# Attention and gated feed-forward in one kernel: two projection units placed ahead of the last token block's first one, and seven early scores instead of three

## The chip, the cores and the metric

The kernel runs on one core of one Trainium2 chip. The metric is device time in microseconds (us) of the whole program: 1323.13 us before the change, the median of three runs (1322.75 to 1323.53).

## The reference

The inputs are x (2048 tokens of 448 numbers), the attention weights wqkv (448 x 1344) and wo (448 x 448), the feed-forward weights W_gate and W_up (448 x 1792) and W_down (1792 x 448), and a gate vector gate_w, all float32. Cut to what matters:

```python
q, k, v = split(x @ wqkv)                      # 16 heads of 28
p = softmax(q @ k.T * 28 ** -0.5)
a = (p @ v) @ wo
b = ((relu(x @ W_gate)) * (x @ W_up)) @ W_down
g = sigmoid((x * gate_w).sum(-1))
out = g * a + (1 - g) * b
```

## The kernel before

Products that need float32 accuracy are made of float32r parts. A weight or activation is split into a high part (a ScalarE copy, `act_high`, L81) and a low part (the rest, a VectorE subtraction, `low`, L87), and each product is eleven matmuls (`TERMS`) that add high and low parts of the four slices of the 448 rows. The order on every engine is written out by hand: the instructions run on each engine in the order in which the code issues them.

**The projection stage** works in units. `qk(tb, c)` (L239) makes 128 columns (chunk c of 7) of q and k for a block tb of 512 tokens (4 blocks): eleven matmuls of 512 columns into a PSUM bank, a high copy on ScalarE and a low part on VectorE into the SBUF tile `st` (3 buffers), and one DMA on POOL's queue that writes both to `qk_d` in DRAM (512 KB). `vproj(tb, t)` (L248) makes v for 128 tokens, eleven matmuls of 450 columns, and ScalarE copies the result and the gate's sum (`zt`) out of PSUM. The bank of a unit comes from `ps_any`, which turns through four: the two banks of the tag `s`, then one of `x` and one of `po`. The weights come in chunks (`load_w` on SP's queue, two buffers; `split_w` on ScalarE and VectorE), the tokens' x in blocks (`load_x`, `split_x`: X0 to X3).

**The code around the change** first issues the units (0,0), (0,1), (1,0), (1,1), (0,2), (2,0) and (3,0) one by one, between the loads and splits. (3,0) is the first that reads X3. Then come the split of the fourth weight chunk, the load of the last one to come (`load_w(3)`), and `load_k(0)` and `load_q(0)`, the eight DMAs on SP's queue that bring head 0's K and Q back from `qk_d`, each copied to four groups of partitions; they need chunk 0 of all four blocks. The rest stands in a list, `mixed`: first (2,1), (1,2) and (3,1), then qk units and vproj units in turn, and it ends with (3,6), v(0,2), (2,6), v(0,3), (1,6), (0,6). Before given places of the list stand two weight splits, the loads of head 1's K and Q, and the spills of x to DRAM (`spill_x`).

From a given unit on, `smax` steps follow the units. `smax(k)` (L130) multiplies 128 queries by 1024 keys in two matmuls into one of two double banks, and VectorE takes the maxima, which the exponentials need. 48 of a total of 512 such steps run in this stage.

**Scores.** `scores(i, j)` (L159) is one matmul of 128 keys (tile i: head i // 16, key tile i % 16) by 512 queries (block j) into one of the two banks of the tag `s`, and the exponential on ScalarE into `PT[i]`, one of five buffers in SBUF, which hold X1, X2 and half of X3 until those have been read for the last time. After each of the last three units one score, s(0,0) to s(0,2), is issued ahead of the `smax` steps. s(0,3) follows behind the list.

**The rounds.** 64 rounds follow, each of which issues 16 scores, `smax` steps (8 in most rounds) and some feed-forward matmuls (`gu_mm`) by a string (`ROUND`: s, m and x), and then `pv` for four key tiles: 4 x 4 narrow matmuls that multiply the exponentials by v. Round 0 has no feed-forward matmuls; its scores are those of the tiles 1 to 4. After the rounds come the rest of the feed-forward part, the output projection and the down projection.

The list as it is built before:

```python
        units = [(qk, 2, 1), (qk, 1, 2), (qk, 3, 1), (qk, 2, 2), (qk, 3, 2)]
        units += [(qk, tb, c) for c in range(3, NQ) for tb in range(NB - 1, -1, -1)]
        vs = [(vproj, tb, t) for tb in range(NB - 1, -1, -1) for t in range(4)]
        mixed = units[:3]
```

Of the kernel before, what the change touches and what calls it, by code (L numbers as in the profile page):

```python
# [27 lines left out]
NB = 4  # L28
# [3 lines left out]
VC = D + 2  # L32
NQ = 2 * D // P
WARM = 13


LEAD = 24
# [18 lines left out]
def gated_mix_kernel(ctx, tc, x, wq, wo, wgu, wd, out):  # L56
# [8 lines left out]
    def f32(ap):  # L65
        return ap.bitcast(F32)

    def ps_s(name):
        return psum.tile([P, TB], F32, tag="s", bufs=2, name=name)
# [4 lines left out]
    def ps_o(name):  # L74
        return psum.tile([P, TB], F32, tag="po", bufs=1, name=name)

    def ps_x(name):
        return psum.tile([P, TB], F32, tag="x", bufs=1, name=name)

    def act_high(dst, src):  # L80
        nc.scalar.activation(dst, src, AF.Copy)  # L81
# [4 lines left out]
    def low(dst, src, high):  # L86
        nc.vector.tensor_tensor(dst, src, f32(high), op=OP.subtract)  # L87
# [19 lines left out]
    def p_slot(name, dt=F32):  # L107
        return vp.tile([P, 4, TB], dt, name=name, tag="P", bufs=PB + 1)
# [9 lines left out]
    def load_k(h):  # L118
        for r in range(4):
            nc.sync.dma_start(f32(K[h % 3])[DH * r:DH * (r + 1)], qk_d[r % 2, 2 * DH * h:2 * DH * h + DH, :])  # L120

    def load_q(h):
        Q[h] = q_slot(f"Q_{h}").rearrange("p j t -> p (j t)")
        for r in range(4):
            nc.sync.dma_start(f32(Q[h])[DH * r:DH * (r + 1)], qk_d[r // 2, 2 * DH * h + DH:2 * DH * (h + 1), :])
# [4 lines left out]
    def smax(k):  # L130

        h, u, half = maxima[k]
        if u == 0 and half == 0:
            MX[h] = keep.tile([P, 32], F32, name=f"mx_{h}", tag="mx", bufs=2)
        ps = ps_w(f"sm_{k}")
        for c in range(2):
            k0 = (half * 2 + c) * TB
            nc.tensor.matmul(ps[:, c, :], Q[h][:GD, u * P:(u + 1) * P], K[h % 3][:GD, k0:k0 + TB],  # L138
                             start=True, stop=True)
        nc.vector.tensor_reduce(MX[h][:, 2 * u + half:2 * u + half + 1], ps, axis=AX.XY, op=OP.max)  # L140
        if u == NK - 1 and half == 1:
            M[h] = keep.tile([P, 16], F32, name=f"m_{h}", tag="m", bufs=2)
            nc.vector.tensor_reduce(M[h], MX.pop(h).rearrange("p (a b) -> p a b", b=2), axis=AX.X, op=OP.max)
# [15 lines left out]
    def scores(i, j):  # L159
        h, kt = divmod(i, NK)  # L160
        if j == 0:
            PT[i] = p_slot(f"P_{i}")
        ps = ps_s(f"s_{i}_{j}")
        nc.tensor.matmul(ps, K[h % 3][:GD + 2, kt * P:(kt + 1) * P], Q[h][:GD + 2, j * TB:(j + 1) * TB],  # L164
                         start=True, stop=True)
        nc.scalar.activation(PT[i][:, j], ps, AF.Exp, scale=SCALE)  # L166
# [3 lines left out]
    def xf(tb, b):  # L170
        return X[tb][b // 4][:, b % 4]


    with tc.tile_pool(name="qkv", bufs=1) as pa:
        W = pa.tile([P, 7, 2 * D + VC], F32R, name="W")

        def load_w(c):
            c0, c1 = c * 2 * GD, (c + 1) * 2 * GD if c < G + 1 else 2 * D + VC
            wr = pa.tile([P, 4, 2 * GD + 2], F32, name=f"wr_{c0}", tag="wr", bufs=2)[:, :, :c1 - c0]
            nc.sync.dma_start(wr, wq[:, :, c0:c1])  # L180
            return wr, c0, c1

        def split_w(wr, c0, c1):

            ways = [(W[:, :, c0:c1], wr)]
            if c0 < 2 * D:
                w, r = (ap.rearrange(f"p c {n} -> p c a j d", a=2, j=4)
                        for ap, n in ((W[:, :, c0:c1], "(j a d)"), (wr, "(a j d)")))
                ways = [(w[:, :, a], r[:, :, a]) for a in range(2)]
            for w, r in ways:  # L190
                act_high(w[:, 0:3], r[:, 0:3])
                low(w[:, 3:6], r[:, 0:3], w[:, 0:3])
            for w, r in ways:
                act_high(w[:, 6], r[:, 3])
                low(w[64:, 6], r[64:, 3], w[64:, 6])
# [34 lines left out]
        def spill_x(tb, r):  # L230
            nc.gpsimd.dma_start(x_d[tb, r], f32(X[tb][r]))
# [3 lines left out]
        def ps_any(name):  # L235
            turn[0] += 1
            return (ps_s, ps_s, ps_x, ps_o)[turn[0] % 4](name)

        def qk(tb, c, terms=TERMS):  # L239
            ps = ps_any(f"qk_{tb}_{c}")  # L240
            for n, (a, b) in enumerate(terms):
                nc.tensor.matmul(ps, W[:, a, c * P:(c + 1) * P], xf(tb, b), start=(n == 0), stop=(n == NT - 1))  # L242
            st = pa.tile([P, 2, TB], F32R, name=f"st_{tb}_{c}", tag="st", bufs=3)
            act_high(st[:, 0], ps)
            low(st[:, 1], ps, st[:, 0])
            nc.gpsimd.dma_start(qk_d[:, c * P:(c + 1) * P, tb * TB:(tb + 1) * TB].rearrange("r d t -> d r t"), f32(st))
# [20 lines left out]
        ps = ps_o("warm_ps")  # L267
        for n in range(WARM):
            nc.tensor.matmul(ps, warm[:, :P], warm, start=True, stop=True)
# [26 lines left out]
        w4 = load_w(4)  # L296
        qk(2, 0)
        w5 = load_w(5)
        qk(3, 0)
        split_w(*w4)  # L300
        w3 = load_w(3)
        load_k(0)
        load_q(0)

        units = [(qk, 2, 1), (qk, 1, 2), (qk, 3, 1), (qk, 2, 2), (qk, 3, 2)]
        units += [(qk, tb, c) for c in range(3, NQ) for tb in range(NB - 1, -1, -1)]
        vs = [(vproj, tb, t) for tb in range(NB - 1, -1, -1) for t in range(4)]
        mixed = units[:3]
        units = units[3:]
        while units or vs:  # L310
            mixed += units[:1] + vs[:1]
            units, vs = units[1:], vs[1:]
        m, first = 0, 8
        spills = {16 + 3 * k: (NB - 1 - k // 2, k % 2) for k in range(6)}
        for n, (f, *a) in enumerate(mixed):
            if n == 1:
                split_w(*w5)
            if n == 3:
                split_w(*w3)
            if n == 6:  # L320
                load_k(1)
                load_q(1)
            if n in spills:
                spill_x(*spills[n])
            f(*a)
            if n >= len(mixed) - 3:
                scores(0, n + 3 - len(mixed))
            while m < 2 * LEAD and n >= first and m < (n + 1 - first) * 2 * LEAD / (len(mixed) - first):
                smax(m)
                m += 1  # L330
                if m == 2 * NK + 3:
                    smax_end(0)
# [59 lines left out]
    NI = H * NK  # L392
# [61 lines left out]
    fetch_f(1)  # L454
    load_k(2)
    load_q(2)
    scores(0, NB - 1)
    for r in range(NR):
        h, q = divmod(r, NK // PB)
        order = ROUND if r < LAST_M else LATE  # L460
        todo = list(range(nxt, min(nxt + (0 if r == 0 else 1 if r < LAST_M else 2), 2 * done)))
        nxt += len(todo)
        if r in X_ROUNDS:
            load_x_split(*X_ROUNDS[r])

        if q == 0 and h and h + 2 < H:
            load_k(h + 2)
            load_q(h + 2)
        if r == 1:
            gates()  # L470
        if r == 2:
            pack_wo()
        if r < LAST_M and m in range(2 * NK, len(maxima), 2 * NK):
            smax_end(m // (2 * NK) - 1)
        if r == LAST_M:
            smax_end(H - 1)
        if h and q == 1:
            row_sums(h - 1)
            spread(h - 1)
        if h and q == 2:  # L480
            normalise(h - 1)
        ns = nx = 0
        for o in order:
            if o == "s":
                i, j = PB * r + 1 + ns // NB, ns % NB
                if i < NI:
                    scores(i, j)
                ns += 1
            elif o == "m":
                smax(m)  # L490
                m += 1
            elif nx < NT * len(todo):
                i, half = divmod(todo[nx // NT], 2)
                if nx % NT == 0:
                    ps = ps_x(f"gu_{i}_{half}") if r < LAST_M else ps_w(f"gu_{i}_{half}")[:, 0]
                gu_mm(ps, i, half, nx % NT)
                nx += 1
                if nx % NT == 0:
                    (spill_h if half else relu)(i, ps)

        ready = min(nxt + (2 if r + 1 < LAST_M else 3), 2 * done + 2)
        while parts < ready:
            split_f(parts // 2, pool_low, (parts % 2,))
            parts += 1
            if parts % 2 == 0:
                fetch_f(parts // 2 + 1)
        if r == LAST_M:
            wor = load_wo()
        for i in range(PB * r, PB * (r + 1)):
            pv(i)  # L510
            if i == NI - NK // 2:
                split_wo(wor)
# [105 lines left out]
    n = todo.index((gate_up, (NB - 1) * NF))  # L618
# [50 lines left out]
```

## Time and profile before

| What | Value |
|---|---|
| Median of three runs | 1323.13 us |
| The profiled execution's own time | 1323.03 us |
| Its span, first to last instruction | 1321.3 us |
| TensorE busy (PE) | 1313.3 us, 99% |
| VectorE (DVE), ScalarE (ACT) | 815.3 us (62%), 772.6 us (58%) |
| GpSimd (POOL) | 307.0 us, 23% |
| Granted TensorE clock | 1.00 |
| The projection stage | up to about 142 us |
| Round 0 | about 142 to 156 us |

One execution was recorded. PE is the matmuls, PEld the weight loads beside them, SPq and POOLq the issuing of DMAs on the queues of SP and POOL. A row of the timeline gives the start and the length of a run of equal instructions in us, the engine, the line, the tiles written and read, how many there are, and in brackets how long the engine was idle before it and what ended that. Ends of matmuls are modelled, and one row may overlap the next. A row of the windows gives the busy time of each engine in that stretch with its instructions in brackets, then the granted clock, the share of the DMA engines that was busy, and GB/s. A row of the waits gives who waited for whom, the time in total, how often, and the longest.

### The profile page before, as it was taken

What the parts mean: (1) busy time and instruction counts of PE and PEld (TensorE: products, weight loads), DVE (VectorE), ACT (ScalarE), POOL (GpSimd) and SP (SyncE); (2) the same over time, 40 slices, a digit from 0 to 9 for tenths busy, and PEclk for the clock granted to TensorE, in tenths of its full rate; (3) what the DMA queues carried; (4) which work ended last, traced back from release to release, by engine and by line L of the source; (5) the groups of instructions that cost most, each with busy time, mean ns of one, the idle gap of its engine ahead of it and who ended that gap; (6) DMA issues with size and microseconds to landing.
All of it is one profiled execution on the core that took longest, in us unless ns stands there. A gap on an engine that the chain in (4) does not pass through costs nothing.

```text
span 1321.3 us, 17544 instructions
## 1 busy us (share of the span) xinstructions
PE 1313.3 (99%) x6689; PEld 894.3 (68%) x6689; DVE 815.3 (62%) x859; ACT 772.6 (58%) x1454; POOL 307.0 (23%) x434
## 2 busy tenths in 40 slices
PE   9999999999999999999999999999999999999998
PEld 5888656656656566566566566565655788888997
DVE  6567867767767767677677677677600456633342
ACT  5212667767767777777677677677788332322121
POOL 3111112131121212222221221312325332301120
PEclk9999999999999999999999999999999999999999
DMA  8744622313223151331324313231122674433432
GB/s 298 263 171 180 175 62 61 81 48 99 56 71 88 40 152 57 89 88 40 88 86 123 77 51 81 61 92 32 50 91 79 209 265 149 163 121 120 133 113 78
DMA packets 50013, 144.67 MB, mean 109 GB/s; under 512 B 9544, under 2 KB 16648, under 8 KB 44808
## 3 DMA queue, kind: packets, MB, share of 16 engines
q1 hardware_dynamic: 33640, 96.70, 25.5%
q0 software_dynamic: 16288, 46.84, 10.2%
q8 instruction: 53, 0.87, 0.3%
q14 instruction: 32, 0.26, 0.1%
HBM read 99.96 MB, written 43.93 MB: 109 GB/s over the span
## 4 chain that ended last, share of the span: by engine, by line
PE 98%; DMA 1%; ACT 0%; DVE 0%; issue 0%; SPq 0%; ACTq 0%
PE gu L374 22%; PE s L164 20%; PE sm L138 19%; PE po L400 17%; PE acc L586 10%; PE qk L242 4%; PE v L251 3%; PE wo L538 3%; DMA xr<-x 1%; DMA qk_d<-st 1%; PE mt L148 0%; ACT X L81 0%; DVE X L87 0%; ACT st L81 0%; ACT P L166 0%
## 5 line engine op out<-in xcount | busy, mean ns | idle before, releaser
L140 DVE TENSOR_REDUCE mx<-sm 128x1 f32<-128x1024 f32 x512 | 606.5, 1219 | 174.9 <-PE sm L138 171.9
L166 ACT ACTIVATE P<-s 128x512 f32<-128x512 f32 x1024 | 583.1, 596 | 168.6 <-PE s L164 109.3
L164 PE MATMUL s<-Q,K 114*128 114x512 f32 x1024 | 419.5, 410 | 0.5 <-ACT P L166 0.5
L138 PE MATMUL sm<-K,Q 112*128 112x512 f32 x1024 | 323.4, 399 | 0.2
L164 PEld LDWEIGHTS s<-Q,K 114*128 114x128 f32 x1024 | 192.1, 188 | 146.8 <-ACT P L166 83.1
L374 PE MATMUL gu<-XF,wg 128*128 128x512 f32 x924 | 270.8, 395 | 0.0
L400 PE MATMUL po<-P,V 128*32 128x512 f32 x2048 | 233.0, 595 | 0.0
L138 PEld LDWEIGHTS sm<-K,Q 112*128 112x128 f32 x1024 | 189.6, 189 | 45.6 <-DVE mx L140 9.9
L374 PEld LDWEIGHTS gu<-XF,wg 128*128 128x128 f32 x924 | 174.6, 189 | 34.1 <-issue 0.8
L90 POOL TENSOR_TENSOR wg<-wgr,wg 128x384 fp32r<-128x384 f32 (+1 forms) x105 | 95.8, 914 | 283.3 <-ACT wg L81 187.5
L400 PEld LDWEIGHTS po<-P,V 128*32 128x32 f32 x2048 | 60.0, 109 | 131.0 <-issue 130.7
L586 PE MATMUL acc<-WD,hh 128*128 128x448 f32 x672 | 141.7, 367 | 0.0
L586 PEld LDWEIGHTS acc<-WD,hh 128*128 128x128 f32 x672 | 126.2, 188 | 12.8
L389 POOL DMA_DIRECT2D h_d<-h x56 | 31.4, 562 | 394.6 <-DVE h L383 188.4
L383 DVE TENSOR_TENSOR h<-gu,rl 128x512 f32<-128x512 f32 x56 | 38.4, 686 | 132.1 <-ACT rl L380 71.1
L380 ACT ACTIVATE rl<-gu 128x512 f32<-128x512 f32 x56 | 33.3, 594 | 128.0 <-PE gu L374 128.0
L374 PE MATMUL gu<-X,wg 128*128 128x512 f32 x308 | 108.0, 395 | 0.0
L87 DVE TENSOR_TENSOR hh<-hr,hh 128x512 fp32r<-128x512 f32 x56 | 55.3, 988 | 51.8 <-ACT hh L81 51.8
L81 ACT ACTIVATE hh<-hr 128x512 fp32r<-128x512 f32 x56 | 35.1, 628 | 74.3 <-PE acc L586 72.4
L242 PE MATMUL qk<-X,W 128*128 128x512 f32 x308 | 76.5, 398 | 1.9 <-ACT X L81 1.6
L81 ACT ACTIVATE wg<-wgr 128x384 fp32r<-128x384 f32 x168 | 72.6, 484 | 0.0
L242 PEld LDWEIGHTS qk<-X,W 128*128 128x128 f32 x308 | 57.4, 189 | 18.0 <-ACT X L81 2.6
(56 smaller groups left out, 596.6 us busy)
## 6 DMA issues: line engine op xcount, KB each, us to landing
wgr<-wgu SPq DMA_DIRECT2D x56, 512.0 KB
qk_d<-st POOLq DMA_DIRECT2D x28, 512.0 KB, 3.7
K<-qk_d SPq DMA_DIRECT2D x64, 224.0 KB
Q<-qk_d SPq DMA_DIRECT2D x64, 224.0 KB
h_d<-h POOLq DMA_DIRECT2D x56, 256.0 KB, 2.3
hr<-h_d SPq DMA_DIRECT2D x56, 256.0 KB
x_d<-X POOLq DMA_DIRECT2D x6, 1024.0 KB, 5.1
XF<-x_d SPq DMA_DIRECT2D x6, 1024.0 KB
```

Of the source, the lines that this page charges most:

```text
L81: nc.scalar.activation(dst, src, AF.Copy)
L87: nc.vector.tensor_tensor(dst, src, f32(high), op=OP.subtract)
L90: nc.gpsimd.tensor_tensor(dst, src, f32(high), op=OP.subtract)
L138: nc.tensor.matmul(ps[:, c, :], Q[h][:GD, u * P:(u + 1) * P], K[h % 3][:GD, k0:k0 + TB], start=True, stop=True)
L140: nc.vector.tensor_reduce(MX[h][:, 2 * u + half:2 * u + half + 1], ps, axis=AX.XY, op=OP.max)
L164: nc.tensor.matmul(ps, K[h % 3][:GD + 2, kt * P:(kt + 1) * P], Q[h][:GD + 2, j * TB:(j + 1) * TB], start=True, stop=True)
L166: nc.scalar.activation(PT[i][:, j], ps, AF.Exp, scale=SCALE)
L242: nc.tensor.matmul(ps, W[:, a, c * P:(c + 1) * P], xf(tb, b), start=(n == 0), stop=(n == NT - 1))
L251: nc.tensor.matmul(ps[:, :VC], xf(tb, b)[:, t * P:(t + 1) * P], W[:, a, 2 * D:], start=(n == 0), stop=(n == NT - 1))
L374: nc.tensor.matmul(ps, WS[i][:, s, a], xf(i // NF, b), start=(n == 0), stop=(n == NT - 1))
L400: nc.tensor.matmul(PO[h][32 * j:32 * j + 32], V[:, kt, h], PT[i][:, j], start=(kt == 0), stop=(kt == NK - 1))
L586: nc.tensor.matmul(ACC[tb][t][:, :D], hh[:, a, t * P:(t + 1) * P], WD[:, f, b], start=(f == 0 and n == 0), stop=(f == NF - 1 and n == 2))
```

## The change

(2,1) and (1,2) are taken from the head of the list and issued ahead of (3,0). The list is two shorter, and the places in it that are given by number (the first `smax`, the spills, the loads of head 1) are two lower, so they stay at the same units. The two weight splits keep their numbers in the list, 1 and 3, and so stand two units later. The early scores are given by a tuple, `EARLY`: entry k is the distance from the end of the list behind whose unit score k is issued. Behind (2,6) stands s(0,0); behind v(0,3) s(0,1) and s(0,2); behind (1,6) s(0,3) and s(1,0); behind (0,6) s(1,1) and s(1,2). Round 0 leaves out the scores that are there already, the first three of its string, and s(0,3) behind the list goes. The number of all instructions is the same.

```diff
+EARLY = (4, 3, 3, 2, 2, 1, 1)
...
         qk(2, 0)
         w5 = load_w(5)
+        qk(2, 1)
+        qk(1, 2)
         qk(3, 0)
         split_w(*w4)
         w3 = load_w(3)
         load_k(0)
         load_q(0)
 
-        units = [(qk, 2, 1), (qk, 1, 2), (qk, 3, 1), (qk, 2, 2), (qk, 3, 2)]
+        units = [(qk, 3, 1), (qk, 2, 2), (qk, 3, 2)]
...
-        mixed = units[:3]
-        units = units[3:]
+        mixed = units[:1]
+        units = units[1:]
...
-        m, first = 0, 8
-        spills = {16 + 3 * k: (NB - 1 - k // 2, k % 2) for k in range(6)}
+        m, first = 0, 6
+        spills = {14 + 3 * k: (NB - 1 - k // 2, k % 2) for k in range(6)}
...
-            if n == 6:
+            if n == 4:
                 load_k(1)
                 load_q(1)
...
-            if n >= len(mixed) - 3:
-                scores(0, n + 3 - len(mixed))
+            for k in range(len(EARLY)):
+                if EARLY[k] == len(mixed) - n:
+                    scores(*divmod(k, NB))
...
-    scores(0, NB - 1)
     for r in range(NR):
...
-                if i < NI:
+                if len(EARLY) <= i * NB + j < NI * NB:
                     scores(i, j)
```

## The prediction

> **What bounds the kernel now.** A unit (tb, c) is `qk` of token block tb and column chunk c, v(tb, t) a `vproj`, s(i, j) a score, m a `smax` (two matmuls and one VectorE maximum). The page comes first:
>
> ```profile
> PE 1313.3 (99%) x6689; PEld 894.3 (68%) x6689; DVE 815.3 (62%) x859; ACT 772.6 (58%) x1454; POOL 307.0 (23%) x434
> ```
>
> TensorE is busy 99% of the span. Every edit here moves work and removes none, so only TensorE's waiting can change. The table of 10 us windows shows where it waits: a full window holds 46 to 48 matmuls, two in the changed stage hold 36.
>
> ```profile
> 20.00:30.00 10.00, 8.42 (x36) 6.13 (x35) 7.29 (x11) 5.37 (x11) 2.90 (x4) 1.00 1.04 395
> ...
> 50.00:60.00 10.00, 10.00 (x47) 8.41 (x46) 6.53 (x6) 1.81 (x5) 1.30 (x2) 1.00 0.77 279
> ...
> 140.00:150.00 10.00, 9.72 (x36) 5.89 (x35) 9.24 (x10) 7.30 (x14) 1.04 (x2) 1.00 0.47 164
> ```
>
> The first is the wait for the last tokens' x, the second is round 0. The granted clock (1.00) is full in all three. Then the timeline by engine, first the early stretch (start, length, instructions, [idle before <- releaser]):
>
> ```profile
> 10.15 13.63 PE L242 MATMUL qk<-X,W 128*128 128x512 f32 x56 [0.16 <-DVE X L87]
> 25.34 13.30 PE L242 MATMUL qk<-X,W 128*128 128x512 f32 x55 [1.55 <-ACT X L81]
> 38.47 2.42 PE L251 MATMUL v<-W,X 128*128 128x450 f32 x11
> ...
> 50.29 1.10 PE L138 MATMUL sm<-K,Q 112*128 112x512 f32 x4
> 27.73 10.47 PEld L242 LDWEIGHTS qk<-X,W 128*128 128x128 f32 x46 [0.46 <-DVE X L87]
> 24.24 2.00 ACT L81 ACTIVATE X<-xr 128x1024 fp32r<-128x1024 f32 x2
> 25.32 2.36 DVE L87 TENSOR_TENSOR X<-xr,X 128x1024 fp32r<-128x1024 f32 x2 [0.25 <-ACT X L81]
> ```
>
> The 55 matmuls from 25.34 are (3,0), (2,1), (1,2), (3,1) and (2,2). (3,0) waits 1.55 us for the high part of X3 and again, at 27.73, for its low part, done at 27.68.
>
> **The change, part one: two units in front of (3,0).** Matmuls start 0.233 us apart ((38.47 - 27.73)/46), a unit takes 2.56 us. Without waiting, a unit could start at 23.62 (the row's end 23.78, less the 0.16 by which ends trail the next start: 38.64 against 38.47). (2,1) and (1,2) need X2 and X1, long there, and fill the time to 28.74, when X3 has been ready for a microsecond. Five units then end at 36.4 instead of 38.47: **2.1 us gained at this place**, and the first m, 50.29 before, could start at 48.2.
>
> What that triggers: (3,0), the last unit that heads 0 and 1 need, now runs from 28.74 to 31.3 and is copied later still, and everything queued behind it moves.
>
> ```profile
> 29.63 0.60 ACT L81 ACTIVATE st<-qk 128x512 fp32r<-128x512 f32 x1 [1.92 <-DMA qk_d<-st]
> 28.72 0.72 POOL L246 DMA_DIRECT2D qk_d<-st  x1 [2.64 <-DVE st L87]
> DMA to landing us min/median/max: 4.1/4.1/4.1
> 31.25 0.72 POOL L246 DMA_DIRECT2D qk_d<-st  x1 [1.80 <-DVE st L87]
> 30.91 1.28 DVE L87 TENSOR_TENSOR W<-wr,W 128x672 fp32r<-128x672 f32 x2
> 17.36 15.40 SPq L180 DMA_DIRECT2D wr<-wq  x3
> 34.89 1.75 SPq L120 DMA_DIRECT2D K<-qk_d  x4
> ...
> 44.86 3.86 SPq L125 DMA_DIRECT2D Q<-qk_d  x4
> SPq L125 <- DMA Q<-qk_d: 3.4, 4, 1.0
> ```
>
> `st` has three buffers, so a unit's copy waits for the write of the unit three before it. (3,0) is now ninth; its copy waits for the sixth unit's write, issued at 28.72 as before and landed 4.1 us later (the row below it), at 32.8. A copy at 32.9 means a write issued 1.62 us later (29.63 to 31.25), at 34.5, landed in 3.6 more (31.25 to K's issue at 34.89, which waited for it), at 38.1. The K and Q loads of head 0, behind it on SP, issue at **38.1 instead of 34.89**. The third weight load moves too: it follows the split of the fourth, whose low part ends at 32.19 now and near 35.4 after, so it stays 2.7 us ahead of K on SP's queue.
>
> When do K and Q land? Head 1's eight loads each wait for the landing of the one eight earlier (the last row), so the last issue, at 48.4 (44.86 + 3.86 - 0.3), is head 0's last landing: 13.5 us after the first issue, and 1.9 us before the first m. From the other side, a later head's loads with nothing beside them:
>
> ```profile
> 247.84 1.62 SPq L120 DMA_DIRECT2D K<-qk_d  x4
> 249.00:250.00 1.00, 1.00 (x6) 0.68 (x5) 0.84 (x2) 0.81 (x3) 0.00 (x0) 1.00 0.68 229
> ...
> 257.00:258.00 1.00, 1.00 (x5) 0.69 (x5) 1.00 (x2) 0.90 (x3) 0.00 (x0) 1.00 0.66 148
> ```
>
> They move bytes until 258: 10.3 us. After the change the load lands between 48.5 and 51.6. I take 12.4 us, nearer the contended row (the same weight load is ahead, and units still write every 5 us, but the backlog of writes is smaller): 50.5. **So the first m starts at 50.5, not 48.2, and the gain is gone: +0.2 us**, bounds -1.7 to +1.3. Behind that waiting m stand all later units on TensorE; ScalarE's copies and VectorE's maxima follow them, so nothing overtakes it.
>
> The lower bound is not -2.1 because v(3,0) has its own wait: the fifth weight split now follows the copy of (3,1), held to 34.9 by the write issued at 31.25. Two copies and the low part (0.6 + 0.7 + 0.86, half a microsecond overlapped) end near 37.0, and the second matmul of v(3,0) wants it at 36.6: 0.4 us, hidden while the K/Q wait is longer. The third weight split, now behind v(3,0), may cost as much again; hidden likewise.
>
> A rule of the Trainium skill speaks against this number (DMA: Bandwidth & Descriptors, Anatomy of one DMA): about 2.0 us fixed plus bytes at 436 GB/s. As an estimate from that page, the eight loads of 224 KB would land 6.2 us after issue, at 44.3, and the gain would stay. The quiet rows (148 to 229 GB/s) do not agree. The same page of the Trainium skill (Queues, rings and completion order) has one ring per engine for SP's queue, consumed in order, and round robin against other queues; by it the weight load in front and the writes beside delay K, as the 13.5 us against 10.3 suggest.
>
> **Part two: seven scores between the last units.**
>
> ```profile
> 128.78 2.72 PE L242 MATMUL qk<-X,W 128*128 128x512 f32 x11
> 131.54 0.60 ACT L81 ACTIVATE st<-qk 128x512 fp32r<-128x512 f32 x1 [2.89 <-PE qk L242]
> 134.54 0.39 PE L164 MATMUL s<-Q,K 114*128 114x512 f32 x1
> 135.18 0.17 ACT L255 ACTIVATE zt<-v 128x1 f32<-128x1 f32 x1
> 141.47 0.40 PE L164 MATMUL s<-Q,K 114*128 114x512 f32 x1
> 142.17 4.87 ACT L166 ACTIVATE P<-s 128x512 f32<-128x512 f32 x8
> 142.81 0.50 PE L164 MATMUL s<-Q,K 114*128 114x512 f32 x1 [0.25 <-ACT P L166]
> 142.91 10.29 DVE L140 TENSOR_REDUCE mx<-sm 128x1 f32<-128x1024 f32 x9
> 151.30 0.63 PE L138 MATMUL sm<-K,Q 112*128 112x512 f32 x2
> 152.59 3.64 PE L400 MATMUL po<-P,V 128*32 128x512 f32 x32
> ```
>
> Round 0 before: the last unit's matmuls end their turn at 141.47, the first `pv` starts at 152.59, 11.1 us for 36 matmuls that need 8.4. Two loops hold it: ScalarE's exponentials, one per 0.6 us through two score banks, and VectorE's nine maxima back to back (1.13 us apart), the first after the last unit's low half. The ninth m needs the bank of the seventh maximum, done at 142.91 + 6 x 1.134 + 1.22 = 150.9; it starts at 151.30. **At most 0.4 us can come out of round 0 by taking scores away.** And that little is used up: with three scores fewer, the first three m stand together, the third waits for the first maximum (144.1) and ends its turn at 144.8; the 13 scores left take 13 x 0.6 = 7.8 us and end at 152.6, as before. After the last unit: 0, bounds -0.4 and +0.1.
>
> Ahead of it the scores cost. The `s` tag has two banks, shared by units and scores; in the program as built s(0,0) takes the one that v(0,3) gets next, and s(0,2) follows v(0,3) in it.
> - Three more scores stand ahead of the end of (0,6): 3 x 0.233 = 0.70.
> - v(0,3) waits for the exponential of s(0,0). That follows the copy of (2,6) on ScalarE (131.54), so it starts near 132.03 and ends at 132.63; the matmuls before v(0,3) (one score, two m, from 131.34) are through at 132.50. 0.2, and 0.1 for restarting (142.81: 0.50 instead of 0.39): 0.3.
> - s(0,2) waits for the copies out of v(0,3), which end 0.81 after TensorE has left it (135.35 against 134.54); it wants to start 0.23 after. 0.6, and 0.1 for restarting: 0.7. The m behind it and the unit (1,6) wait with it.
>
> Sum **+1.7 us**, bounds +1.3 (round 0's 0.4) and +2.0. The copies of (1,6) and (0,6), the writes and the first weight split of the feed-forward part move with the units and wait for nothing new.
>
> **Sum.** The profiled execution took 1323.03 us (span 1321.3), 0.1 below the median of three. 0.2 + 1.7 = 1.9: **1324.9 us**. A later round has 43 matmuls (10.0 us) and its `pv` against eight maxima (9.1), so TensorE sets its length and the shift stays to the end.
>
> **Rivals.**
> 1. The front's gain survives: K and Q land by 48.6 (under 10.5 us; the quiet rows' 10.3 speaks for it, the 13.5 against). -1.7 + 1.7: 1323.0. The Trainium skill's 6.2 us would give this. 13%.
> 2. Clearly slower: the K/Q load is what the new order makes last. If it takes 13.5 us again the first m starts at 51.6, +1.3; with a tail of +2.0, 1326.3. It decides from 13.2 us on (+1.0 with the forecast tail). For it: the weight load stands as far in front as before. Against: fewer writes in flight. 23%.
> 3. Round 0 is ScalarE's after all: three exponentials less (1.8) outweigh three scores (0.7), the new bank waits vanish, and the front keeps 1.7: 1323.03 - 1.1 - 1.7 = 1320.2. The nine maxima without a gap speak against it. 4%.
>
> **How the numbers follow.** Forecast 60%. About 0.2% (2.6 us) is what a measurement of this kernel can tell from no change; the forecast and rival 1 lie within it: same 73%, slower 23%, faster 4%. The range adds the bounds: -1.7 + 1.3 = -0.4, 1322.6; +1.3 + 2.0 = +3.3, 1326.3.
>
> **What would show it.** (a) No wait of TensorE for ACT X or DVE X near 25 us, v(3,0) near 36.5. (b) K's issue on SP near 38 and a wait of 1 to 2 us before the first m, ended by the loads, at 50.5; a start at 48 to 49 refutes step one. (c) Two short waits around v(0,3), the nine maxima again without gap, and 11 us from the last unit to the first `pv`; under 10.5 us refutes step two.

## The result

The changed kernel takes 1329.93 us (median of five runs, 1329.85 to 1330.97) against 1323.25 us (five runs of the kernel before beside them, 1322.75 to 1323.74): ratio 1.0052, 95% interval 1.0038 to 1.0066. It is **6.7 us slower**; the forecast was +1.9 (1324.9 us), the range ended at 1326.3. The profiled execution took 1330.16 us (span 1328.4), 7.1 more than the profiled one of before. Line numbers of the changed kernel are 2 to 5 higher.

The page first: TensorE is busy 99% as before, with the same number of instructions.

```profile
PE 1315.6 (99%) x6689; PEld 895.6 (67%) x6689; DVE 816.1 (61%) x859; ACT 772.9 (58%) x1454; POOL 307.8 (23%) x434
```

The table of 10 us windows shows where that changed. The last three columns are granted clock, DMA share and GB/s.

```profile
20.00:30.00 10.00, 10.00 (x45) 8.14 (x44) 7.56 (x11) 5.30 (x11) 2.71 (x4) 1.00 1.03 387
...
50.00:60.00 10.00, 6.29 (x21) 4.76 (x20) 2.36 (x2) 1.21 (x3) 0.49 (x1) 0.83 0.92 281
...
150.00:160.00 10.00, 8.74 (x32) 4.68 (x35) 10.00 (x10) 7.06 (x14) 0.73 (x1) 1.00 0.65 197
```

The wait for x near 25 us is gone: 45 matmuls instead of 36 in the first window. The second held 47 and now holds 21, and its clock is no longer 1.00. The timeline of TensorE says which instructions:

```profile
9.98 26.36 PE L244 MATMUL qk<-X,W 128*128 128x512 f32 x111 [0.16 <-DVE X L89]
36.66 0.47 PE L253 MATMUL v<-W,X 128*128 128x450 f32 x1 [0.32 <-ACT W L83]
37.56 2.30 PE L253 MATMUL v<-W,X 128*128 128x450 f32 x10 [0.43 <-DVE W L89]
...
47.94 2.42 PE L253 MATMUL v<-W,X 128*128 128x450 f32 x11
54.07 1.55 PE L140 MATMUL sm<-K,Q 112*128 112x512 f32 x4 [3.71 <-DMA K<-qk_d]
55.42 3.92 PE L244 MATMUL qk<-X,W 128*128 128x512 f32 x11
```

Ten units now run in one row without a gap, and v(3,0) starts at 36.66 instead of 38.47. Then the first m stands 3.71 us before its loads and starts at 54.07 instead of 50.29. The unit behind it takes 3.92 us where one took 2.72, and the m itself 1.55 where it took 1.10: together 1.65 us more, and the rows name no engine as the cause. The windows of half a microsecond show it:

```profile
54.00:54.50 0.50, 0.43 (x2) 0.42 (x3) 0.00 (x0) 0.00 (x0) 0.00 (x0) 1.00 1.11 336
54.50:55.00 0.50, 0.50 (x4) 0.36 (x3) 0.19 (x1) 0.00 (x0) 0.00 (x0) 0.63 0.79 246
55.00:55.50 0.50, 0.50 (x3) 0.41 (x2) 0.50 (x1) 0.00 (x0) 0.00 (x0) 0.50 0.94 328
...
57.50:58.00 0.50, 0.50 (x3) 0.35 (x2) 0.00 (x0) 0.00 (x0) 0.00 (x0) 0.50 0.84 336
58.00:58.50 0.50, 0.50 (x4) 0.41 (x3) 0.00 (x0) 0.00 (x0) 0.00 (x0) 0.96 0.94 369
```

**The granted clock falls to half** at 54.63 (0.63 of the half microsecond from 54.5) and is full again at 58.04: 3.4 us. The loads in the timeline, first on SP's queue, then on POOL the writes of four units, from the sixth to the ninth, which is (3,0), then the third weights' split on ScalarE:

```profile
17.04 19.02 SPq L182 DMA_DIRECT2D wr<-wq  x3
39.33 2.25 SPq L122 DMA_DIRECT2D K<-qk_d  x4
...
50.09 4.17 SPq L127 DMA_DIRECT2D Q<-qk_d  x4
```

```profile
29.47 0.73 POOL L248 DMA_DIRECT2D qk_d<-st  x1 [3.60 <-DVE st L89]
32.06 0.73 POOL L248 DMA_DIRECT2D qk_d<-st  x1 [1.86 <-DVE st L89]
33.31 0.73 POOL L248 DMA_DIRECT2D qk_d<-st  x1 [0.53 <-DVE st L89]
34.55 0.73 POOL L248 DMA_DIRECT2D qk_d<-st  x1 [0.51 <-DVE st L89]
```

```profile
41.77 0.48 ACT L83 ACTIVATE W<-wr 128x336 fp32r<-128x336 f32 x1 [1.27 <-DMA wr<-wq]
```

The third weight load, last of the first row, has been issued at 36.06 (17.04 + 19.02) instead of 32.76 and is waited for until 41.77. (3,0)'s write is issued at 34.55 and landed at 39.33, when K may go: 4.8 us, 3.6 before. The weight load has moved with that write: it is through 1.51 us behind the write's start, as before (31.25 to 32.76). New are the two writes 1.24 and 2.49 us ahead of (3,0)'s; before, the nearest stood 2.53 us ahead (28.72). K and Q take 14.7 us from there to the first m; the last issue of head 1's, at 53.96 (50.09 + 4.17 - 0.3), which follows head 0's last landing, says the same.

Last the end of the projection stage, TensorE and then VectorE:

```profile
134.19 2.72 PE L244 MATMUL qk<-X,W 128*128 128x512 f32 x11
...
138.09 2.53 PE L253 MATMUL v<-W,X 128*128 128x450 f32 x11
140.46 0.39 PE L166 MATMUL s<-Q,K 114*128 114x512 f32 x1
141.31 0.50 PE L166 MATMUL s<-Q,K 114*128 114x512 f32 x1 [0.47 <-ACT zt L257]
...
148.60 0.64 PE L166 MATMUL s<-Q,K 114*128 114x512 f32 x2
...
159.73 3.64 PE L405 MATMUL po<-P,V 128*32 128x512 f32 x32
```

```profile
150.03 10.30 DVE L142 TENSOR_REDUCE mx<-sm 128x1 f32<-128x1024 f32 x9
```

The first row is (2,6), 5.41 later than before (128.78). The first `pv`, at 159.73, is 7.14 later (152.59): the tail cost 1.73. From the last unit's turn (148.60) to it are 11.13 us, 11.12 before, with the nine maxima again back to back.

**The account**, against the same points of before: v(3,0) is 1.8 us earlier; the first m is 3.8 later, so that gain is gone; the clock adds 1.65, which makes 5.4 at (2,6); the tail adds 1.73: 7.1 us, which stays to the end.

### The profile page after: what moved, and what is told of

Same layout as the page of the kernel before. It is cut to its first block, busy times and chain, and to the rows that moved or that the text cites. A ratio compares the mean times of both kernels' runs of the same rounds, so it can differ in the third digit from the quotient of the medians.

```text
span 1328.4 us, 17542 instructions
## 1 busy us (share of the span) xinstructions
PE 1315.6 (99%) x6689; PEld 895.6 (67%) x6689; DVE 816.1 (61%) x859; ACT 772.9 (58%) x1454; POOL 307.8 (23%) x434
## 3 DMA queue, kind: packets, MB, share of 16 engines
q0 software_dynamic: 16288, 46.84, 10.2%
## 4 chain that ended last, share of the span: by engine, by line
PE 94%; DMA 3%; DVE 2%; ACT 1%; issue 0%; POOL 0%; SPq 0%; ACTq 0%; POOLq 0%
PE gu L379 22%; PE s L166 19%; PE sm L140 18%; PE po L405 17%; PE acc L590 10%; PE qk L244 3%; PE wo L542 3%; PE v L253 2%; DMA K<-qk_d 1%; DMA qk_d<-st 1%; DVE mx L142 1%; DMA xr<-x 1%; DVE st L89 0%; ACT st L83 0%; PE mt L150 0%
## 5 line engine op out<-in xcount | busy, mean ns | idle before, releaser
L590 PEld LDWEIGHTS acc<-WD,hh 128*128 128x128 f32 x672 | 126.2, 188 | 12.8
```

The source lines that it names most:

```text
L590: nc.tensor.matmul(ACC[tb][t][:, :D], hh[:, a, t * P:(t + 1) * P], WD[:, f, b], start=(f == 0 and n == 0), stop=(f == NF - 1 and n == 2))
```

## The experiments

The theory after the result was that the front turns its gain into a wait for K and Q, and that the wait costs a second time by the clock; the tail is as forecast. The rival: the clock has another cause, or K and Q take as long as they are given. Each run stands beside runs of the kernel before on the same chip.

**The parts alone.** Part one alone is the changed kernel with three scores between the last units, and s(0,3) right behind the third; part two alone is the old front with seven.

```diff
-EARLY = (4, 3, 3, 2, 2, 1, 1)
+EARLY = (3, 2, 1, 1)
```

> Part one alone: the two units stand ahead of (3,0), the early scores are three as before and s(0,3) comes right behind them. Theory: the first m waits 3.7 us for K and Q (start 3.8 us later than before), the clock drops behind that wait (1.6 us more), and the tail costs nothing: +5.4 us against the kernel before, 1328.6. Rival (the loss needs both parts, because the seven scores meet units that come late): about +2, 1325.

Measured: 1329.16 us against 1323.23, ratio 1.0043 (1.0028 to 1.0058), +5.9.

```profile
47.32 2.42 PE L253 MATMUL v<-W,X 128*128 128x450 f32 x11
54.59 2.05 PE L140 MATMUL sm<-K,Q 112*128 112x512 f32 x4 [4.86 <-DMA Q<-qk_d]
56.43 3.99 PE L244 MATMUL qk<-X,W 128*128 128x512 f32 x11
```

> Part two alone: the units as before, seven scores between the last units. Theory: +1.7 us (three scores ahead of the last unit 0.7, two waits at the score banks 0.9, nothing out of round 0), 1324.9, with the clock at 1.00 throughout. Rival (the loss needs both parts): within 0.5 us of before, or faster by up to 1.1 if round 0 is ScalarE's.

Measured: 1324.59 us, ratio 1.0010 (1.0001 to 1.0020), +1.4; in its trace the tail adds 1.72 (from 2.33 later than before at (2,6), since the third weights landed late ahead of v(3,0), to 4.05 at the first `pv`). The parts add up (5.9 + 1.4 against 6.7), and nearly all of the miss is part one. The same trace shows how firm the 13.5 us of before are, on which the prediction's bound rests. Its front is the old one, and its loads of K and Q are

```profile
36.67 1.77 SPq L122 DMA_DIRECT2D K<-qk_d  x4
47.44 4.16 SPq L127 DMA_DIRECT2D Q<-qk_d  x4
```

From 36.67 to head 1's last issue at 51.3 (47.44 + 4.16 - 0.3), which follows head 0's last landing, are 14.6 us.

**The same wait, filled.** Part one alone with 14 bf16 matmuls on the zero tile of the warm-up ahead of the first m (13 of them are in the trace). They are added work.

```diff
+            if n == first:
+                ps = ps_w("fill")[:, 0]
+                for _ in range(14):
+                    nc.tensor.matmul(ps, warm[:, :P], warm, start=True, stop=True)
```

> As the kernel with part one alone, with 14 added matmuls on zeros (3.0 us at full clock, into a bank that the next m overwrites) between the unit ahead of the first m and that m, so that TensorE works through most of the wait. Theory that the wait itself drops the clock: the granted clock stays at 1.00 after 54 us and 1.6 us come back, +3.8 us against before, though work was added. Rival (the matmuls behind the wait are slow for another reason, such as the transfers beside them): they stay slow and the time stays at +5.4; if the added work is not hidden, more.

Measured: 1327.20 us, ratio 1.0028 (1.0017 to 1.0038): 2.0 us **faster than without the added work**.

```profile
49.73 2.97 PE L336 MATMUL fill<-warm 128*128 128x512 bf16 x13
54.48 1.16 PE L140 MATMUL sm<-K,Q 112*128 112x512 f32 x4 [1.77 <-DMA K<-qk_d]
55.48 2.71 PE L244 MATMUL qk<-X,W 128*128 128x512 f32 x11
```

The first m starts as late as in part one alone (54.48 against 54.59); only the idle time differs, 1.77 against 4.86, and the unit behind takes 2.71 instead of 3.99. So the idle time itself lowers the clock.

**The weight load behind K and Q.** Part one alone; the third weight load is issued behind head 0's loads, its split moves to place 9.

```diff
-        w3 = load_w(3)
         load_k(0)
         load_q(0)
+        w3 = load_w(3)
...
-            if n == 3:
+            if n == 9:
                 split_w(*w3)
```

> As the kernel with part one alone, with the load of the third weight chunk behind head 0's K and Q on SP's queue instead of ahead of them, and its split at place 9 of the list instead of 3. Theory that the weight load in front delays K and Q (their first transfer lands 5.8 us after its issue, 4.6 before the change): they land 1 to 2 us earlier, the wait falls to 1.5 to 2.7 us, the clock holds, and the time is +1 to +3 us. Rival (K and Q are late only because (3,0) is written late, the weight load costs nothing): K's issue near 39.3, landing near 54 and +5.4 as with part one alone.

Measured: 1326.53 us, ratio 1.0024 (1.0014 to 1.0033), 2.6 us less than with the load in front.

```profile
38.27 1.67 SPq L122 DMA_DIRECT2D K<-qk_d  x4
```

```profile
51.59 1.17 PE L140 MATMUL sm<-K,Q 112*128 112x512 f32 x4 [2.31 <-DMA Q<-qk_d]
52.59 4.28 PE L244 MATMUL qk<-X,W 128*128 128x512 f32 x11
```

K is issued at 38.27 (39.54 with the weight load in front, 39.33 in the changed kernel; 38.1 was the forecast), and the first m follows 13.3 us later instead of 15.0 and 14.7. Against these two traces, then, the weight load beside (3,0)'s write and ahead of K costs 1.1 to 1.3 us at the issue of K and 1.4 to 1.7 in the load.

It does not cost that wherever it stands. Before, in part two alone and with one unit in front (below), the same load is through 1.51 us behind (3,0)'s write too, and the write lands in 3.64, 3.70 and 4.24 us; the nearest write ahead of it starts 2.53, 3.46 and 1.21 us earlier. So the long landing goes with both, the weight load behind the write and other writes close in front of it; no run moved the writes alone. And the load of K and Q, from the first issue to the last of head 1's, took 13.5, 14.6 and 13.3 us in these three traces, with the weight load in front in each. That the load in front makes it long is not shown.

That the clock would hold with 2.3 us of waiting did not come true: the unit takes 4.28.

**A later first m.** First with one unit, (2,1), in front and the first m at place 9 of a list one longer; then both units in front, at place 9; three early scores in both.

> One unit, (2,1), ahead of (3,0) instead of two, three early scores, and the smax steps begin at place 9 of the list, two units later than before. Theory (the cost of part one is the wait for K and Q and the clock behind it): one unit covers the wait for X3, the first m comes near 53 us when K and Q have landed, the clock stays at 1.00, and the gain ahead of it reaches the end: 1 to 2 us faster than before, 1321.2 to 1322.2. Rival (the same 48 steps in fewer units make VectorE the bound there, or the weight splits wait as long as X3 did): 1323 or more.

Measured: 1328.38 us, ratio 1.0042 (1.0026 to 1.0059). A miss, and a lesson about the edit:

```profile
40.24 4.05 PE L253 MATMUL v<-W,X 128*128 128x450 f32 x11 [3.88 <-ACT W L83]
```

With the list one longer, place 3, where the third weights are split, comes to lie ahead of v(3,0), as it did before; but their load now lands near 39. v(3,0), which reads the same tile W, waits 3.88 us for that split, and its eleven matmuls take 4.05 instead of 2.42: another wait with a lowered clock behind it.

```diff
-        m, first = 0, 6
+        m, first = 0, 9
```

> Both units ahead of (3,0) as in the changed kernel, three early scores, and the smax steps begin three units later than before (place 9 of the shorter list). Theory: the first m comes near 55.5 us, after K and Q (54 to 54.5), the clock holds, and what the two units gain is kept but for the waits of v(3,0) and v(3,1) for their weights: 0.5 to 1.8 us faster than before, 1321.4 to 1322.7; against part one alone 6 us. Rival (late K and Q are not what costs): 1327 or more.

Measured: 1323.86 us, ratio 1.0004 (0.9995 to 1.0014): 5.5 us better than with the m at place 6 (+0.4 against +5.9), and no difference to before that can be measured. The first m starts at 57.12 without waiting, the clock is full. The trace says where the 2.1 us of X3 go: v(3,0) and v(3,1) wait for the weight splits (v(3,0) starts 1.59 earlier than before, v(3,1) 0.80, v(3,2) only 0.47), and the 48 m stand over 26 places instead of 29, so two stand at more places in a row; between 60 and 130 us, eight pairs of m take about 1.40 us instead of 1.09, and four before: 2.5 us lost instead of 1.2. The profiled execution ends 0.9 later than before.

**Weight load late, split early, one place later.** Both units in front, the weight load behind K and Q, the fifth weights split at place 0 (ahead of (3,1)), the third at place 9, the first m at 7.

> Part one with the third weight load behind K and Q, the split of the fifth weights ahead of (3,1), and the first m one place later (7 instead of 6). Theory: the loss was the m standing ahead of its loads. With K and Q landing near 51.5, as with the late weight load alone (38.3 + 13.2), and the m now due near 51.4, TensorE waits under 1 us for them, the clock stays full, and of the 2.1 us gained at X3 some 0.4 goes to the weight splits ahead of v(3,0), 0.4 to the denser m and 0.2 to chance: 1 us faster than before, 1322.3. Rival: the K/Q load takes what room it is given (14.7 us again behind 38.3 = 53.0): a wait of 1.6 us, the gain gone, 1323.5 or more.

Measured: 1322.45 us against 1322.75, ratio 0.9997 (0.9988 to 1.0006); span of the profiled execution 1320.7.

```profile
36.23 2.41 PE L253 MATMUL v<-W,X 128*128 128x450 f32 x11
...
51.69 1.17 PE L140 MATMUL sm<-K,Q 112*128 112x512 f32 x4 [0.97 <-DMA Q<-qk_d]
52.69 2.41 PE L253 MATMUL v<-W,X 128*128 128x450 f32 x11
```

v(3,0) has all of the gain now (38.47 - 36.23 = 2.2 us), the wait is 0.97 us, the clock holds. The best of the family, and still not to be told from the kernel before.

**What makes K and Q slow?** Three runs take neighbours away from them, each from the late weight load on. First v(3,0) to v(3,3) in a row, which write nothing, so that two unit writes lie beside the loads instead of four:

```diff
-        mixed = units[:1]
-        units = units[1:]
+        mixed = units[:2] + vs[:4] + units[2:5]
+        units, vs = units[5:], vs[4:]
+        mixed += vs[:1]
+        vs = vs[1:]
```

> Part one with the third weight load behind K and Q, as in the run of that alone, and besides v(3,0) to v(3,3) in a row behind (2,2), with the qk units (3,2), (3,3), (2,3) behind them. v units write nothing to DRAM, so only two writes, of (3,1) and (2,2), lie beside head 0's loads, instead of four. Theory: the unit writes lengthen the loads. They take 11 us or less from the first issue (38.3) to the last landing, the first m starts by 50 with a wait under 1 us, and the clock stays full. Rival: the weights and the writes of (3,0) and (3,1) made the length, or the loads' own pace: 13 us again, a wait over 2 us and a lowered clock.

Measured: 1329.88 us, ratio 1.0055 (1.0042 to 1.0068). K issued at 39.10, first m at 52.30: 13.2 us, against 13.3 with the late weight load alone. The theory of the unit writes fails in this form; the weight load and head 1's loads follow K and Q in both. (Some 2.4 us of this run's loss are later: the third split, at place 9, now stands right ahead of a v unit, which waits for it at 62 us.)

Then the third weight load and head 1's loads go to POOL's queue, later, with the early split:

```python
             if n == 7:
                 w3 = load_w(3, nc.gpsimd)
             if n == 9:
                 load_k(1, nc.gpsimd)
             if n == 11:
                 load_q(1, nc.gpsimd)
             if n == 13:
                 split_w(*w3)
```

> Part one with the first m at its place (6), the split of the fifth weights ahead of (3,1), and everything that shares SP's queue with head 0's loads taken away from them: the third weight load and head 1's loads go to POOL's queue and are issued behind the sixth, seventh and eighth place of the list, after 47 us. Only the unit writes lie beside the loads. Theory, the third after weights and writes alone: the loads are lengthened by what is queued behind them on SP, head 1's above all. They take 10.3 to 11.3 us as a later head's do alone, from 38.3 to 48.6 to 49.6, the first m waits under 1 us, the clock stays full, and of the 2.1 us 1.5 are kept: 1321.3 against 1322.8. Rival: with the unit writes beside them the loads take 13.2 us whatever stands behind them: a wait of 2.3 us or more, a lowered clock, 1326.

Measured: 1326.42 us, ratio 1.0019 (1.0010 to 1.0028). From 38.41 to 52.32, 13.9 us: what stands behind the loads on SP does not lengthen them either. This theory falls too.

Last, besides, four units write later:

```diff
+        LATER, later = [(3, 1), (2, 2), (3, 2), (3, 3)], []
...
+            if (tb, c) in LATER:
+                later.append((tb, c))
+                return
...
```

> As the run with nothing behind head 0's loads on SP, and besides the units (3,1), (2,2), (3,2) and (3,3) write nothing where they stand: their places in qk_d are written by later units, beside those units' own writes, with the later unit's tile (so heads 2 to 7 get wrong K and Q; the number of operations on every engine is the same). Theory, the last one left: the loads and the writes share the DMA engines, which are 0.9 busy from 34 to 54 us in every one of these runs; each 512 KB write beside the loads lengthens them by 0.9 to 1.2 us ((13.9 - 10.3) for three to four writes). Without them the loads take 10.3 to 11 us from 38.4, land by 49.4, the first m waits under 0.7 us, the clock stays full, and of the 2.1 us at X3 1.5 or more are kept: 1321.8 against 1323.3. Rival: the loads are slow at this place for another reason: 13 us or more again, a wait over 2 us, a lowered clock, 1326.

Measured: 1326.29 us, ratio 1.0021 (1.0012 to 1.0030). TensorE, then the windows of half a microsecond:

```profile
45.96 2.42 PE L260 MATMUL v<-W,X 128*128 128x450 f32 x11
51.17 2.04 PE L140 MATMUL sm<-K,Q 112*128 112x512 f32 x4 [2.80 <-DMA Q<-qk_d]
53.02 4.64 PE L246 MATMUL qk<-X,W 128*128 128x512 f32 x11
```

```profile
49.00:49.50 0.50, 0.00 (x0) 0.00 (x0) 0.00 (x0) 0.02 (x1) 0.00 (x0) 1.00 0.57 131
49.50:50.00 0.50, 0.00 (x0) 0.00 (x0) 0.00 (x0) 0.00 (x0) 0.00 (x0) 1.00 0.15 33
50.00:50.50 0.50, 0.00 (x0) 0.00 (x0) 0.00 (x0) 0.00 (x0) 0.00 (x0) 0.90 0.05 16
50.50:51.00 0.50, 0.00 (x0) 0.00 (x0) 0.00 (x0) 0.00 (x0) 0.00 (x0) 0.50 0.00 0
51.00:51.50 0.50, 0.33 (x1) 0.36 (x2) 0.00 (x0) 0.00 (x0) 0.00 (x0) 0.50 0.00 0
...
57.00:57.50 0.50, 0.50 (x4) 0.38 (x3) 0.00 (x0) 0.00 (x0) 0.00 (x0) 0.78 0.00 0
```

12.8 us from the first issue (38.36) to the first m, the shortest of these runs but not the 10.3 to 11 expected; the weight load, free of the unit writes on POOL's queue, was issued early, at 35.85, and landed only 6.7 us later, so something was beside the loads after all. The windows show something else. The bytes are all but through at 50.0 (33 GB/s, then 16, the last 8 KB by 50.1), and the first m starts at 51.17: **a good microsecond lies between the last bytes and the release of who waits.** The "10.3 us" of the quiet rows was the end of the bytes (258 - 247.84 is 10.2); as a time to the first m it would have been near 11.3, an estimate from these two. The remaining 1.5 us are open: no run had neither a weight load nor unit writes beside the loads.

**Does VectorE hold round 0?** The forecast of the tail said that three scores fewer in round 0 bring nothing, since the nine maxima set its length. Part two alone, and the kernel before, each with those nine maxima over 128 of the 1024 keys (the other seven eighths are left out of them):

```diff
-..., ps, axis=AX.XY, op=OP.max)
+..., ps[:, :, :64] if 2 * LEAD - 2 < k < 2 * LEAD + 8 else ps, axis=AX.XY, op=OP.max)
```

> Part two alone, and the nine maxima from the last unit through round 0 taken over the first 64 columns of each half (128 of 1024 keys; the rest of those maxima is left out), so that VectorE needs about 0.2 us for each instead of 1.13. Theory (VectorE's nine maxima keep round 0 from gaining by three fewer scores): from the end of the last unit's turn to the first pv 9.7 us instead of 11.1. Rival (score banks and ScalarE set it, the maxima stand beside): 11.1 as before.

> The kernel before (with s(0,3) directly behind s(0,2)), with the same nine maxima over 128 of 1024 keys, the rest left out. Theory (with all scores still in round 0 ScalarE's loop is as long as VectorE's): 10.8 us from the end of the last unit's turn to the first pv, 0.3 less than before; so three scores fewer are worth 1.0 us where VectorE does not bind. Rival (VectorE alone sets round 0): 9 us or less.

Measured, in one profiled execution of each: TensorE from the end of the last unit's turn to the first `pv`; part two alone, then the kernel before:

```profile
143.23 0.64 PE L166 MATMUL s<-Q,K 114*128 114x512 f32 x2
...
153.04 3.64 PE L403 MATMUL po<-P,V 128*32 128x512 f32 x32
```

```profile
141.86 0.64 PE L166 MATMUL s<-Q,K 114*128 114x512 f32 x2
...
152.69 3.64 PE L403 MATMUL po<-P,V 128*32 128x512 f32 x32
```

9.81 and 10.83 us; with full maxima both are 11.1. Without VectorE's loop the three scores would have brought 1.0 us; with it they bring nothing. The step is shown.

## Why the prediction was wrong, step by step

- **X3's wait goes: right.** 2.1 us gained there; v(3,0) at 36.66 (36.5 forecast), with the 0.75 us of waiting for the fifth weights that the prediction put at 0.4 and hid behind the m.
- **K is issued at 38.1: wrong by 1.2** (39.33). The write was issued as forecast, 34.55 against 34.5, but by luck: the sixth unit's write, for which (3,0)'s copy waits, was issued 0.75 us later than taken (29.47, not 28.72) and landed 0.8 faster (3.3 us, not 4.1). The step that failed is the landing of (3,0)'s own write: 3.6 us was taken from before, and it took 4.8. In the row of before the weight load follows just as closely, but no write stands closer than 2.53 us ahead; the new order puts one at 1.24. With that load behind K and the same writes ahead, the landing takes 3.7 to 3.9 us and the issue is at 38.27 to 38.41 (39.10 in the one that also started its front late); behind the write on POOL's own queue the load does not delay it either (38.36).
- **K and Q take 12.4 us: wrong by 2.3** (14.7, above even the bound of 13.5). The bound was one execution of before; with the same front, part two alone shows 14.6. 1.4 to 1.7 us go when the weight load stands behind K and Q, but with it in front the traces show anything from 13.3 to 15.1 us to head 1's last issue, so what sets the length stays open. The reason for going below 13.5, a smaller backlog of writes, finds little support: two writes fewer beside the loads made 13.2 of 13.3; without any, but with the weight load beside them, 12.8 of 13.9. The other end of the range was mis-read: bytes that end at 10.2 us release nobody before about 11.3, so a value between the ends was some 0.5 too low.
- **The price of a wait: missing from the sum.** The prediction began with "only TensorE's waiting can change" and priced every microsecond that the first m waits at one microsecond; the clock was left out. Here 3.7 us of waiting cost 1.65 more at half clock. Rival 2, "clearly slower", had the right mechanism (the load is what the new order makes last), but its price stopped at 1326.3 for this reason and the two above.
- **The tail: right.** +1.73 against +1.7: v(0,3) 0.2 late, s(0,2) 0.47 behind the copies out of v(0,3), three scores ahead of the last unit, and nothing back in round 0.
- The Trainium skill's figure (6.2 us for the eight loads, DMA: Bandwidth & Descriptors, Anatomy of one DMA) was set aside; rightly, since the shortest seen here to a first m is 12.8. That section fits single DMAs issued from GpSimd, and these go out on SP's queue.

In numbers, forecast to measured: 0.21 + 1.23 + 2.34 = 3.78 at the first m; + 1.65 clock; + 1.73 tail; 7.1.

## What to carry to other kernels

If work is put in front of a transfer that a later instruction needs, follow the transfer with everything that is issued beside it: here other writes came to stand close ahead of the write that K and Q wait for, beside a weight load that had been there all along, and the landing went from 3.6 to 4.8 us. Do not take the length of one execution's transfer for a bound: the same front showed 13.5 and 14.6 us. Price a wait of TensorE at its length and, if it is longer than the 1.77 us that still left the clock full here, at 1.5 to 2.8 us on top (from the first m to the next pair 5.02 us in the run with nothing behind the loads and 6.32 in the run without writes, 3.49 before). Look for other work to stand there: the first m three places later in the list was worth 5.5 us. And a gain ahead of a fixed landing time is worth nothing until what follows it is moved as well: with all of it moved, this one was still within 0.1% of before.

## What the runs showed of the hardware

**How long half clock lasts.** In every trace with a lowered clock it stays low for 3.4 or 6.8 us: 3.4 in five of them, as from 54.63 to 58.04 in the changed kernel; 6.8 in part one alone (52.37 to 59.20) and in the run without writes (50.40 to 57.22), where the fall comes while TensorE still waits. Waits of 0.97, 1.55 and 1.77 us left the clock full; seven waits, from 2.31 us (weight load late) to 4.86 (part one alone), did not. The Trainium skill (TensorE: Matmul & The Clock Gate, What's actually happening) describes this: activity is watched in windows of 3413 ns that run on by themselves, half rate after an idle window, full rate after a busy one. The 3.4 and 6.8 us agree with one and two such windows. That a whole window must be idle does not agree: in the run without writes the clock had fallen after 2.0 us of idling (from 48.4), and a wait of 2.31 us was enough in another. So the advice of the Trainium skill in the same page (Why this matters for your kernels), no gaps over about 3 us, is not strict enough here. If the windows do not move with the program, the same wait may cost in one execution and not in the next. The eleven runs of the kernel without writes would fit that, from 1324.03 us with a mean clock of 1.000 to 1328.79 with 0.997, but only one of them was profiled, so whether their waits were alike is not shown.

**From the last bytes to the release** there is about 1 us (50.1 to 51.2 above), read from the run without writes, in which nothing else moved bytes at that time.
